# Second feed-forward product in groups of 512 tokens over both batches, with its activations in four fixed buffers, in a fused attention and MLP kernel

## The chip, the cores and the metric

The kernel runs on one core of one Trainium2 chip. The metric is the device time of one execution in microseconds (us). Before the change three runs took 455.62, 456.00 and 456.24 us, so the median is 456.0 us.

## The reference, cut to what matters

Three blocks follow each other: a decaying linear attention, a token-mixing low-rank product with a ReLU feed-forward (`ch`), and a gated MLP. B=2 batches, S=768 tokens, 512 features, 2048 hidden features.

```python
state = gamma * state + einsum('bhd,bhe->bhde', k[:, :, t], v[:, :, t])
y[:, :, t] = scale * einsum('bhd,bhde->bhe', q[:, :, t], state)
...
xt = x.transpose(0, 2, 1)
h = xt @ U @ V
u = x + h.transpose(0, 2, 1)
ch = np.maximum(u @ w_ch1, 0.0) @ w_ch2
x = u + ch
...
h = np.maximum(x @ w_in, 0.0)
u, v = h[..., :d_ff // 2], h[..., d_ff // 2:]
v_s = einsum('ts,bsd->btd', w_spatial, layernorm(v)) + b_spatial[None, :, None]
out = (u * v_s) @ w_out
```

## The kernel before, in words

Activations lie feature-major: `X[b]` is a tile of 128 partitions by four feature blocks by 768 tokens. T = 384 tokens is half a batch. A product in full precision is made of three matmuls (`triple`): each operand is split into a high and a low part of type fp32r, and high times high, high times low and low times high are added in one PSUM bank. A high part is a cast on ScalarE, a low part a subtraction on VectorE or GpSimd.

**Attention.** It runs per pair of heads, eight pairs (four for each batch). A pair loads `q`, `k` (feature-major, named `h` in the load list) and `v`, and for most pairs also `kk`, the same keys token-major; pairs in `TURNED` instead transpose `k` on TensorE (`scale`, L414) and scale the result on its way out of PSUM (L419). `scores` makes the score banks `sc`, masks them into `pt` on VectorE (L451) or on ScalarE and GpSimd (`VIA`, L448 and L449), and forms the chunk states `ds` and their scan `s` (L461). `mix` makes `x` from `pt`, `v`, `q` and `s`; `turn` transposes `x` (`t`, L502), `down` and `up` are the low-rank product (`g`, `gt`, `hu`).

**Feed-forward.** The 2048 hidden features are taken in eight steps `m` of 256. `ch1(m, b)` computes them for one batch; from m = 1 on as a `quad`, seven products of half-size operands (named 1, 5, 6, 7, 2, 4, 3) in four banks qa, qb, qc and qd. Its results leave PSUM in `store(i, h)`, where i is the half of the 256 features and h the half of the tokens. Three of the four are first added to a helper `y` on VectorE (L756), then get their ReLU in place on ScalarE (L757), are cast to the high part (L758) and subtracted for the low part (L759). The fourth goes from the bank with one ScalarE and one VectorE instruction (L753, L754). Each (m, b, i, h) has its own activation tile `a`, taken from the pool "a" of 36 buffers. `ch2(m, b)` then multiplies them with `w2`: for each half h and each of four feature blocks d there are two triples of 384 columns in one bank `acc`, and VectorE adds the bank to `X` (L784).

**The rest.** `gate_u`, `gate_v`, `spatial` and `final` follow with products of 384 and 256 columns.

**What sets the order.** The program first records operations with costs and keys in a `Plan`. `settle` arranges them repeatedly with an event model of the engines, and `give_out` then emits them in the order found. So each engine's program order, also that of SyncE's loads, is fixed in advance by the model's costs. Where the model sees TensorE idle for over 0.5 us before 60 us, `give_out` emits filler matmuls of 384 bf16 columns (`spend`) ahead of the next one; WARM = 11 of them open the program. `SEQ` is the sequence (0,0), (0,1), (1,0), ... (7,1) of (m, b); `ch2` of one element is keyed across the span of the next.

All matmuls are issued at L348 except the transposes.

Of the kernel before, what the change touches and what calls it, by code (L numbers as in the profile page):

```python
# [43 lines left out]
class Plan:  # L44
# [48 lines left out]
    def arrange(self, sizes):  # L93
# [16 lines left out]
        free["D"] = FIRST  # L110
# [189 lines left out]
def pe(n, passes=1):  # L300
    return passes * (10.8 + 0.4219 * n), False
# [3 lines left out]
POOLS = {"a": 36, "w": 24, "raw": 2, "y": 2, "t": 2, "r": 6, "st": 6, "s": 2, "g": 2, "sm": 2, "ps": 8}  # L305
# [16 lines left out]
SUM0, SUM1 = 80.8, 106.2  # L322
VIA = {0: (2,), 1: (), 2: (), 3: (0, 1, 2, 3), 4: (2, 3), 5: (1, 2, 3), 6: (1, 2), 7: (1, 3)}
# [3 lines left out]
TURNED = (0,)  # L327
SEQ = [(m, b) for m in range(NM) for b in range(B)]

STEP = {n: 6 * pe(n)[0] / 1000 for n in (T, DM // 2)}  # L330
# [5 lines left out]
def tile_kernel(ctx: ExitStack, tc: tile.TileContext, a, out: bass.AP):  # L336
    nc = tc.nc
    const = ctx.enter_context(tc.tile_pool(name="const", bufs=1))
    psm = ctx.enter_context(tc.tile_pool(name="psm", bufs=1))
# [16 lines left out]
    sc_t = const.tile([P, 2 * H + NP * (NCH - 1)], F32, name="scales")  # L356
# [13 lines left out]
    X = [const.tile([P, ND, S], F32, name=f"x{b}") for b in range(B)]  # L370

    def xs(b, d, h):
        return X[b][:, d, h * T:(h + 1) * T]
# [54 lines left out]
    def scores(i):  # L428
        b, p = divmod(i, NP)
        for e in range(2):  # L430
            pt_t[i, e] = Buf("a", [P, NCH, P], F32, f"pt{i}{e}")
        for h in range(2):
# [9 lines left out]
            for e in range(2):  # L442
                m = msc[:, 2 * p + e:2 * p + e + 1]

                def pt(e=e, h=h):
                    return pt_t[i, e].t[:, TC * h:TC * h + TC, :]
                if (2 * h + e) in VIA[i]:
                    op({"A": (582, False)}, lambda E, pt=pt, x=sc[e], m=m: E.activation(pt(), x.t, AF.Copy, scale=m), r=[sc[e], "sc"], w=[(pt_t[i, e], h)])  # L448
                    op({"G": gss(T)}, lambda E, pt=pt: E.tensor_mul(pt(), pt(), tri()), r=[(pt_t[i, e], h), TRI], w=[(pt_t[i, e], h)])  # L449
# [614 lines left out]
```

## Time and profile before

| what | before |
|---|---|
| median of three runs | 456.0 us |
| the profiled execution's own time | 454.77 us |
| span of the profiled execution | 453.1 us |
| TensorE busy | 447.2 us (99%) |
| VectorE busy | 396.3 us (87%) |
| ScalarE busy | 257.0 us (57%) |
| GpSimd busy | 126.7 us (28%) |

The span runs from the first to the last instruction; 1.7 us of the profiled time lie around it. "Busy" counts a matmul from its start to its modelled end, and matmuls overlap, so two busy matmuls may follow each other in less than the sum of their durations; the distance between starts is what tells TensorE's pace. The times in all rows are from the span's start. The granted TensorE clock is reported as 1.00 for the whole span.

### The profile page before, as it was taken

Reading aid. Unit: us, or ns where it says so; the run is one execution under the profiler, and the core shown is the slowest. Engines: PE = TensorE matmul, PEld = TensorE weight load, DVE = VectorE, ACT = ScalarE, POOL = GpSimd, SP = SyncE. Lnnn points to the kernel's source line nnn. Section 1 sums busy time; section 2 is a strip of 40 time slices with the busy share of each in tenths; the row PEclk is TensorE's granted clock in tenths of the full one; section 3 lists DMA queues with packets and bytes.
Section 4 is the critical chain, followed back from the end, with each engine's and each line's share of the span. In section 5 each row is a group of like instructions: output and inputs, shape, how many; then the busy total and the mean of one; then the engine's idle time right before and its main releaser. Section 6 shows DMA issues by size and latency. Waiting matters only on the chain.

```text
span 453.1 us, 8442 instructions
## 1 busy us (share of the span) xinstructions
PE 447.2 (99%) x3235; PEld 434.8 (96%) x3235; DVE 396.3 (87%) x847; ACT 257.0 (57%) x526; POOL 126.7 (28%) x112
## 2 busy tenths in 40 slices
PE   9999999999999999999999999999999999999996
PEld 6888799999999999999999999999999999999996
DVE  2767899999999999989888797899997999999843
ACT  3376775673766675754563554566566778353410
POOL 3076763463834242322131012101410001150000
PEclk9999999999999999999999999999999999999999
DMA  8995412320353341433122012000112022000033
GB/s 299 399 399 192 139 50 93 93 94 10 90 179 95 94 138 50 150 110 107 54 93 81 13 48 87 19 1 1 35 36 72 0 94 93 2 1 1 1 139 139
DMA packets 14151, 42.95 MB, mean 95 GB/s; under 512 B 1696, under 2 KB 2592, under 8 KB 14112
## 3 DMA queue, kind: packets, MB, share of 16 engines
q1 hardware_dynamic: 13968, 42.41, 27.3%
q8 instruction: 25, 0.41, 0.4%
q14 instruction: 14, 0.11, 0.1%
q10 hardware_dynamic: 144, 0.02, 0.0%
HBM read 39.27 MB, written 3.15 MB: 94 GB/s over the span
## 4 chain that ended last, share of the span: by engine, by line
PE 92%; DVE 5%; ACT 1%; POOL 0%; issue 0%; DVEq 0%; ACTq 0%
PE acc L348 29%; PE pz L348 8%; PE x L348 4%; PE c L348 4%; PE sc L348 3%; PE t L502 1%; PE ds L348 1%; DVE s21t L556 1%; DVE f21t L562 1%; PE idle L348 1%; DVE f21b L562 1%; DVE pz L862 1%; DVE x L863 1%; PE q10a L348 1%; PE q50a L348 0%; PE qo11d L348 0%
## 5 line engine op out<-in xcount | busy, mean ns | idle before, releaser
L348 PE MATMUL acc<-a,hw 128*128 128x384 f32 x512 | 130.1, 334 | 0.0
L348 PEld LDWEIGHTS acc<-a,hw 128*128 128x128 f32 x512 | 92.5, 188 | 0.3 <-DVE a L759 0.3
L348 PE MATMUL acc<-a,lw 128*128 128x384 f32 x256 | 85.5, 334 | 0.0
L784 DVE TENSOR_TENSOR x<-acc,x 128x384 f32<-128x384 f32 x128 | 69.3, 550 | 7.5 <-PE acc L348 6.9
L600 POOL TENSOR_TENSOR rw<-rw,tw 128x512 int32<-128x512 int32 x32 | 50.7, 1586 | 82.8 <-DVE rw L598 69.8
L348 PEld LDWEIGHTS acc<-a,lw 128*128 128x128 f32 x256 | 48.1, 188 | 0.0
L757 ACT ACTIVATE y<-y 128x384 f32<-128x384 f32 x42 | 22.0, 523 | 36.9 <-DVE y L756 36.7
L595 ACT ACTIVATE yw<-raww 128x512 f32<-128x512 f32 x32 | 21.6, 676 | 19.7 <-DVE rw L598 15.0
L759 DVE TENSOR_TENSOR a<-y,a 128x384 fp32r<-128x384 f32 x39 | 23.7, 608 | 2.9 <-ACT a L758 2.5
L598 DVE SCALAR_TENSOR_TENSOR rw<-yw,rw 128x512 uint32<-128x512 uint32 x32 | 23.1, 723 | 0.0
L596 ACT ACTIVATE tw<-raww 128x512 int32<-128x512 uint32 x32 | 21.6, 674 | 1.1 <-POOL rw L600 1.0
L600 POOL TENSOR_TENSOR rwo<-rwo,two 128x512 int32<-128x512 int32 x4 | 5.4, 1341 | 60.0 <-DVE rwo L598 60.0
L758 ACT CAST a<-y 128x384 fp32r<-128x384 f32 x42 | 21.5, 513 | 1.0
L449 POOL TENSOR_TENSOR pt<-pt,shared 128x384 f32<-128x384 f32 x14 | 14.2, 1036 | 18.7 <-ACT pt L448 18.6
L348 PE MATMUL pz<-ws,vn 128*128 128x384 f32 x108 | 19.0, 334 | 0.0
L348 PE MATMUL pz<-hws,vn 128*128 128x384 f32 x72 | 18.9, 334 | 0.0
L348 PEld LDWEIGHTS pz<-ws,vn 128*128 128x128 f32 x108 | 18.8, 188 | 0.0
L600 POOL TENSOR_TENSOR rwv<-rwv,twv 128x512 int32<-128x512 int32 x4 | 5.3, 1333 | 30.9 <-DVE rwv L598 12.6
L608 ACT CAST hw<-rw 128x512 fp32r<-128x512 f32 x18 | 11.1, 618 | 4.5 <-POOL rw L600 4.2
L348 PE MATMUL sc<-q,k 64*128 64x128 f32 x192 | 13.4, 281 | 0.0
L597 DVE TENSOR_SCALAR rw<-yw 128x512 uint32<-128x512 uint32 x32 | 13.4, 423 | 0.0
L348 PEld LDWEIGHTS sc<-q,k 64*128 64x128 f32 x192 | 11.7, 187 | 1.6 <-issue 0.7
(1080 smaller groups left out, 1260.6 us busy)
## 6 DMA issues: line engine op xcount, KB each, us to landing
raww<-in_w SPq DMA_DIRECT2D x32, 512.0 KB, 3.6
q<-in_qT SPq DMA_DIRECT2D x8, 384.0 KB, 7.8
k<-in_kT SPq DMA_DIRECT2D x8, 384.0 KB, 7.9
v<-in_v SPq DMA_DIRECT2D x8, 384.0 KB, 7.7
kk<-in_k SPq DMA_DIRECT2D x7, 384.0 KB, 7.8
raws<-in_ws SPq DMA_DIRECT2D x6, 384.0 KB, 3.0
out_y<-out SPq DMA_DIRECT2D x6, 384.0 KB, 2.4
rawwu<-in_wu SPq DMA_DIRECT2D x4, 512.0 KB, 3.5
```

The costliest lines, as they stand in the source:

```text
L348: nc.tensor.matmul(o, l, r, start=start, stop=stop, skip_group_check=True)
L449: op({"G": gss(T)}, lambda E, pt=pt: E.tensor_mul(pt(), pt(), tri()), r=[(pt_t[i, e], h), TRI], w=[(pt_t[i, e], h)])
L595: op({"A": c}, lambda E: E.activation(y.t, words(1).bitcast(F32), AF.Copy, scale=2.0 ** -112), r=whole, w=[y])
L596: op({"A": c}, lambda E: E.activation(t.t, words(0), AF.Copy, scale=2.0 ** -29), r=whole, w=[t])
L597: op({"V": vone(n)}, lambda E: E.tensor_single_scalar(r.t, y.t.bitcast(U32), 3, ALU.logical_shift_left), r=[y], w=[r])
L598: op({"V": vss(n)}, lambda E: E.scalar_tensor_tensor(r.t, y.t.bitcast(U32), 0x80000000, r.t, ALU.bitwise_and, ALU.bitwise_or), r=[y, r], w ...
L600: op({"G": gss(n)}, lambda E: E.tensor_tensor(o().bitcast(I32), r.t.bitcast(I32), t.t, ALU.add), r=[r, t], w=[tok])
L608: op({"A": acp(DM)}, lambda E: E.copy(h.t, f(r.t)), r=[r], w=[h])
L757: op({"A": (525, False)}, lambda E: E.activation(y[0](), y[0](), AF.Relu), r=[y[1]], w=[y[1]])
L758: op({"A": acp(T)}, lambda E: E.copy(t.t[:, 0, :], y[0]()), r=[y[1]], w=[(t, 0)])
L759: op({"V": vss(T), "G": gss(T)}, lambda E: E.tensor_sub(t.t[:, 1, :], y[0](), f(t.t[:, 0, :])), r=[y[1], (t, 0)], w=[(t, 1)])
L784: op({"V": vps(T)}, lambda E, o=o, v=xs(b, d, h): E.tensor_add(v, o.t, v), r=[o, ("X", b, d, h)], w=[("X", b, d, h)])
```

## The change

- `ch2` works on groups. For m = 0 to 6 there are three groups of 512 tokens: group 0 is the first 512 tokens of batch 0, group 1 the first 512 of batch 1, group 2 the last 256 of both. Each group and feature block has two triples of 512 columns and one VectorE addition of 512 columns. For m = 7 the four halves of 384 tokens stay.
- The activations of a step lie in four fixed buffers, `a0h`, `a0l`, `a1h` and `a1l`, which hold both batches and are reused by every m. They come from a new pool "b" of 4, shared with the attention's `pt`, which becomes one tile per pair.
- ReLU goes straight from `y` to the high part on ScalarE. The cast is gone; the low part is max(y, 0) minus high, in one VectorE instruction (no longer GpSimd).
- Group 0 of m is keyed into the span of `ch1(m, 1)`, groups 2 and 1 into that of `ch1(m + 1, 0)`, each `LAGS` = 3.9 after the span's begin.
- Pair 1 joins `TURNED`: its `kk` is no longer loaded, and TensorE transposes its `k`. Load order and load keys change, and the pools too (a 29, b 4, w 21, raw 3).
- The planner multiplies the costs of VectorE, ScalarE and GpSimd by `PAD` = 1.02, lets TensorE begin at 0.78, and emits fewer fillers per hole.
- The last stored half tile is added in two pieces of 192 columns, whose stores go out on the ScalarE and the SyncE queue.

```diff
-POOLS = {"a": 36, "w": 24, "raw": 2, ...}
+POOLS = {"a": 29, "b": 4, "w": 21, "raw": 3, ...}
...
-LOADS = 'q0 h0 v0 k1 gs h1 v1 q1 q2 h2 k2 v2 q3 h3 k3 v3 U V0 V1 w10 w11 q4 ...'.split()
+LOADS = "q0 h0 v0 gs h1 v1 q1 q2 h2 k2 v2 q3 h3 k3 v3 U V0 V1 w10 w11 q4 ...".split()
...
+LAGS = 3.9
+PAD = 1.02
+HEAD, LATER = 16, 9.3
-TURNED = (0,)
+TURNED = (0, 1)
...
-                    idle(int((o.start - free - 200.0) / 320.0) + 1, target[-1])
+                    idle(int((o.start - free - 100.0) / 320.0), target[-1])
...
-    A = {}
+    A = [[Buf("b", [P, B, S], F32R, f"a{i}{x}") for x in "hl"] for i in range(2)]
...
             op({"V": vps(T)}, lambda E: E.tensor_add(y[0](), src.t, add[0]()), r=[src, add[1]], w=[y[1]])
-            op({"A": (525, False)}, lambda E: E.activation(y[0](), y[0](), AF.Relu), r=[y[1]], w=[y[1]])
-            op({"A": acp(T)}, lambda E: E.copy(t.t[:, 0, :], y[0]()), r=[y[1]], w=[(t, 0)])
-            op({"V": vss(T), "G": gss(T)}, lambda E: E.tensor_sub(t.t[:, 1, :], y[0](), f(t.t[:, 0, :])), r=[y[1], (t, 0)], w=[(t, 1)])
+            op({"A": (525, False)}, lambda E: E.activation(hi(), y[0](), AF.Relu), r=[y[1]], w=[th])
+            op({"V": vss(T)}, lambda E: E.scalar_tensor_tensor(lo(), y[0](), 0.0, f(hi()), ALU.max, ALU.subtract), r=[y[1], th], w=[tl])
...
-    def ch2(m, b):
-        for h in range(2):
+    def ch2(m, parts):
+        for part in parts:
+            n = T if isinstance(part, tuple) else DM
+            at = {0: (0, slice(0, n)), 1: (1, slice(0, n)), 2: (slice(0, B), slice(n, S))}[part] if n == DM else ...
             for d in range(ND):
-                o = bank([P, T], f"acc{m}{b}{h}{d}")
+                o = bank([P, n], f"acc{m}{d}{part}"...)
                 for i in range(2):
-                    x = A[m, b, i, h]
+                    xh, xl = A[i]
                     triple(o, i == 0, i == 1, n, ...)
-                op({"V": vps(T)}, lambda E, o=o, v=xs(b, d, h): E.tensor_add(v, o.t, v), ...)
+                op({"V": vps(n)}, add, r=[o] + toks, w=toks)
...
-        prev = None
-        for cur in SEQ + [None]:
-            if cur:
-                ch1(*cur)
-            if prev:
-                ch2(*prev)
-            prev = cur
+        for m, b in SEQ:
+            groups = ([(0, 0), (0, 1)] if m == NM - 1 else [0]) if b else [2, 1]
+            if (m, b) != (0, 0):
+                plan.key = ch[m, b] + LAGS
+                ch2(m if b else m - 1, groups)
+            ch1(m, b)
+        ch2(NM - 1, [(1, 0), (1, 1)])
```

**How the order moves, first place: TensorE in the attention of the first two pairs.** Before, behind the first `x` bank of pair 0 (`pt` tiles 187 and 191 belong to pair 0, `kk_126` to pair 1):

```order
L348 LDWEIGHTS const-bfloat16-1.0
L348 MATMUL x_226<-const-bfloat16-1.0 128x384
L348 LDWEIGHTS const-bfloat16-1.0
L348 MATMUL x_226<-const-bfloat16-1.0 128x384
L348 MATMUL x_226<-pt_187,v_122 64x128
...
L348 MATMUL ds_241<-v_135,kk_126 64x64 x10
```

At the same place in the change (`pt_182` is pair 0, `k_126` and `kk_228` pair 1):

```order
L350 MATMUL x_202<-pt_182,v_120 64x128 x6
L417 MATMUL k_216<-shared,k_126 128x128 x3
L417 MATMUL k_222<-shared,k_126 128x128 x3
L350 MATMUL x_231<-pt_182,v_120 64x128 x6
L350 MATMUL ds_244<-v_130,kk_228 64x64 x10
```

Six transposes of pair 1's keys stand where two fillers stood. Of fillers there are 21 before (11 opening ones, 5 ahead of the first transposes, 2 here, 2 among pair 1's scores, 1 ahead of `hu`) and 15 in the change (11, 2, and 2 ahead of `hu`).

**Second place: TensorE from the end of `ch1(5, 1)` to the first reader of its activations.** `q51d` is the bank of product 3, the quad's last, whose `store(0, 1)` writes half h = 1 of batch 1. Before, `acc_3165` reads half h = 0 (`a_3113`, `a_3154`); the first reader of half 1 comes 46 rows later, after three more banks and three products of `ch1(6, 0)`:

```order
L348 MATMUL q51d<-f01b_1051,hsbw_2412 128x384 x2
L348 MATMUL q51d<-f01b_1051,lsbw_2437 128x384
L348 MATMUL acc_3165<-a_3113,hw_2498 128x384 x2
L348 MATMUL acc_3165<-a_3113,lw_2530 128x384
L348 MATMUL acc_3165<-a_3154,hw_2626 128x384 x2
L348 MATMUL acc_3165<-a_3154,lw_2645 128x384
L348 MATMUL q60a<-f00b_689,hw16a 128x384 x2
```

In the change `acc_2847` still reads group 0, and `acc_2893`, the first bank of group 2, reads what `q51d` has just given:

```order
L350 MATMUL q51d<-f01b_1068,hsbw_2333 128x384 x2
L350 MATMUL q51d<-f01b_1068,lsbw_2437 128x384
L350 MATMUL acc_2847<-a1h,hw_2447 128x512
L350 MATMUL acc_2847<-a1l,hw_2447 128x512
L350 MATMUL acc_2847<-a1h,lw_2489 128x512
...
L350 MATMUL q60d<-f00t_919,lsaw_2598 128x384
L350 MATMUL acc_2893<-a0h,hw_2433 128x512
L350 MATMUL acc_2893<-a0l,hw_2433 128x512
```

Twelve matmuls of 384 columns (`q60a` and `q60d`) and three of 512 stand between the two.

**Third place: VectorE behind the same `q51d`, in the change.** `y_2753` is the quad's helper, `a0l` the low part that `acc_2893` reads:

```order
L759 TENSOR_TENSOR y_2753<-q51d,y_2753 128x384
L796 TENSOR_TENSOR x<-acc_2847,x 128x512
L761 SCALAR_TENSOR_TENSOR a0l<-y_2753,a0h 128x384
L641 TENSOR_TENSOR lsaw_2882<-saw_2647,hsaw_2845 128x512
```

Between the addition that ends the product and the low part stands one addition of 512 columns to `X`. Over the whole program VectorE has 801 rows for 841, ScalarE 487 for 523.

## Rows read from the trace of the kernel before

**Rows 1.** The page, part 1: busy us (share of the span) and instructions.

```profile
PE 447.2 (99%) x3235; PEld 434.8 (96%) x3235; DVE 396.3 (87%) x847; ACT 257.0 (57%) x526; POOL 126.7 (28%) x112
```

**Rows 2.** TensorE's two waits at the end of the attention: us in total, times, longest.

```profile
PE c L348 <- POOL lw L609: 0.6, 1, 0.6
PE hu L348 <- DVE gt L489: 0.5, 1, 0.5
```

**Rows 3.** Timeline of TensorE, 384 columns, then 256: start us, length us, what.

```profile
224.80 0.51 PE L348 MATMUL q51a<-f01b,hw15a 128*128 128x384 f32 x2
...
229.48 0.51 PE L348 MATMUL q51b<-f01t,hsaw 128*128 128x384 f32 x2
351.78 0.28 PE L348 MATMUL qv02c<-hsbwv,f10t 128*128 128x256 f32 x1
...
352.86 0.28 PE L348 MATMUL qv10a<-hwv0a,f11b 128*128 128x256 f32 x1
```

**Rows 4.** The page, part 5: busy us, mean ns of one, idle before.

```profile
L348 PE MATMUL acc<-a,hw 128*128 128x384 f32 x512 | 130.1, 334 | 0.0
...
L784 DVE TENSOR_TENSOR x<-acc,x 128x384 f32<-128x384 f32 x128 | 69.3, 550 | 7.5 <-PE acc L348 6.9
...
L759 DVE TENSOR_TENSOR a<-y,a 128x384 fp32r<-128x384 f32 x39 | 23.7, 608 | 2.9 <-ACT a L758 2.5
L598 DVE SCALAR_TENSOR_TENSOR rw<-yw,rw 128x512 uint32<-128x512 uint32 x32 | 23.1, 723 | 0.0
```

**Rows 5.** Windows: PE, PEld, DVE, ACT, POOL busy (x), clock, DMA share, GB/s.

```profile
40.00:57.00 17.00, 16.41 (x272) 12.97 (x269) 15.35 (x32) 14.04 (x29) 13.63 (x14) 1.00 0.41 126
100.00:130.00 30.00, 30.00 (x175) 30.00 (x174) 29.40 (x60) 17.81 (x35) 16.27 (x14) 1.00 0.25 71
```

**Rows 6.** Timeline of TensorE from the start, and of six later transposes.

```profile
0.84 3.68 PE L348 MATMUL idle<-const-bfloat16-1.0 128*128 128x384 bf16 x11 [0.84 <-PEq L1053]
4.32 1.81 PE L348 MATMUL k<-const-bfloat16-1.0 128*128 128x384 bf16 x5
5.92 1.08 PE L414 MATMUL k<-shared,k 128*128 128x128 f32 x6
6.92 1.61 PE L348 MATMUL sc<-q,k 64*128 64x128 f32 x24
...
11.79 1.61 PE L348 MATMUL sc<-q,k 64*128 64x128 f32 x24
...
41.91 0.87 PE L502 MATMUL t<-shared,x 128*128 128x128 f32 x6
```

**Rows 7.** The chain that ended last, near 19 us: start us, us, what.

```profile
19.02 1.65 PE t L502 x12
```

**Rows 8.** SyncE's loads: issues, and us to landing (of the first k, then of q at 4.10).

```profile
1.24 0.42 SPq L354 DMA_DIRECT2D k<-in_kT  x1
...
DMA to landing us min/median/max: 3.6/3.6/3.6
...
4.10 0.80 SPq L354 DMA_DIRECT2D q<-in_qT  x1
...
DMA to landing us min/median/max: 7.6/7.6/7.6
...
8.08 0.33 SPq L354 DMA_DIRECT2D v<-in_v  x1
...
29.51 0.33 SPq L354 DMA_DIRECT2D kk<-in_k  x1
```

**Rows 9.** Timeline around one activation, VectorE, ScalarE and GpSimd.

```profile
164.25 1.45 POOL L600 TENSOR_TENSOR rw<-rw,tw 128x512 int32<-128x512 int32 x1 [1.85 <-ACT y L489]
164.47 1.79 DVE L609 TENSOR_TENSOR lw<-rw,hw 128x512 fp32r<-128x512 f32 x1
...
170.84 0.54 DVE L756 TENSOR_TENSOR y<-q31d,y 128x384 f32<-128x384 f32 x1
...
171.41 0.53 ACT L757 ACTIVATE y<-y 128x384 f32<-128x384 f32 x1 [0.84 <-DVE y L756]
```

More of the change, by code (lines that the diff above doesn't have):

```diff
@@ L109, in arrange @@
         dma, sent = 0.0, 0
-        free["D"] = FIRST
+        free["D"], free["P"] = FIRST, FIRST
         def add(o):
@@ L368, in ident @@
         return shared.t[:, NP + 1, :]
-    X = [const.tile([P, ND, S], F32, name=f"x{b}") for b in range(B)]
+    X = const.tile([P, B, ND, S], F32, name="x")
     def xs(b, d, h):
-        return X[b][:, d, h * T:(h + 1) * T]
+        return X[:, b, d, h * T:(h + 1) * T]
     q_t, k_t, kk_t, v_t, pt_t, s_t, xtok, g_t = ({} for _ in range(8))
@@ L429, in scores @@
         b, p = divmod(i, NP)
-        for e in range(2):
-            pt_t[i, e] = Buf("a", [P, NCH, P], F32, f"pt{i}{e}")
+        pt_t[i] = Buf("b", [P, 2, NCH, P], F32, f"pt{i}")
         for h in range(2):
@@ L529, in run @@
                         mm(u[z].t, g_t[b].t[rows, :], vst.t[rows, h * T:(h + 1) * T], True, True)
[L530 removed]
+                op({"P": (380, "up")}, run, r=[g_t[b], (vst, h)], w=u)
                 for z in range(2):
@@ L869, in store @@
             t, d, cut = ts[i], 2 * m + i, slice(h * T, (h + 1) * T)
+            if (b, m, i, h) == (B - 1, 1, 0, 1):
+                for z, q in enumerate("ED"):
+                    sl, to = slice(z * T // 2, (z + 1) * T // 2), slice(h * T + z * T // 2, h * T + (z + 1) * T // 2)
+                    op({"V": vps(T // 2)}, lambda E, sl=sl, to=to: E.tensor_add(t.t[:, to], src.t[:, sl], add[0]()[:, sl]), r=[src, add[1]], w=[(t, h, z)])
+                    dma(lambda to=to: out[b, d * P:(d + 1) * P, to], lambda to=to: t.t[:, to], P * T * 2, r=[(t, h, z)], eng=q)
+                return
             if add is None:
@@ L906, in tile_kernel @@
         at = [AT0 + STEP0 * i for i in range(NP)] + [AT1 + STEP1 * i for i in range(NP)]
-        loads = {x: k - 100.0 for k, x in enumerate(LOADS)}
+        loads = {x: k - 100.0 if k < HEAD else LATER + (k - HEAD) * 1.0 for k, x in enumerate(LOADS)}
         for i in range(2 * NP):
@@ L929, in tile_kernel @@
                 up(i // NP)
-        ch, need = {}, {}
+        ch, need, span = {}, {}, {}
         t = CH0
-        for n, (m, b) in enumerate(SEQ):
+        for m, b in SEQ:
             ch[m, b] = t
             need.setdefault(m, t)
-            t += 15 * STEP[T] + (CH1 if n == 0 else 0)
-        gu = t
+            span[m, b] = 7 * STEP[T] + (CH1 if (m, b) == (0, 0) else 0 if (m, b) == (0, 1) else 8 * STEP[T] if m == NM - 1 and b else (8, 4)[b] * STEP[DM])
+            t += span[m, b]
+        gu = t + 8 * STEP[T]
         for m in range(NM):
@@ L943, in tile_kernel @@
             for z in range(2):
-                weight("w2", 2 * m + z, need[m] + (8 + z) * STEP[T] - LEAD, loads.get(f"w2{2 * m + z}"))
+                weight("w2", 2 * m + z, ch[m, 1] + z * STEP[T] - LEAD, loads.get(f"w2{2 * m + z}"))
         for m in range(2):
@@ L955, in tile_kernel @@
             operands(0, b, "t1 t2 t3 t4")
-        prev = None
-        for cur in SEQ + [None]:
-            if cur:
-                plan.key, plan.pace = ch[cur], 15 / 7
-                ch1(*cur)
-            if prev:
-                plan.key, plan.pace = ch[cur] if cur else gu - 7 * STEP[T], 15 / 8 if cur else 1
-                ch2(*prev)
-                if prev[0] == NM - 1:
-                    operands(1, prev[1], LAST)
-            prev = cur
+        for m, b in SEQ:
+            groups = ([(0, 0), (0, 1)] if m == NM - 1 else [0]) if b else [2, 1]
+            if (m, b) != (0, 0):
+                plan.key = ch[m, b] + LAGS
+                plan.pace = (span[m, b] - LAGS) / (4 * len(groups) * STEP[T if m == NM - 1 and b else DM])
+                ch2(m if b else m - 1, groups)
+            plan.key, plan.pace = ch[m, b], span[m, b] / (7 * STEP[T])
+            ch1(m, b)
+        operands(1, 0, LAST)
+        plan.key, plan.pace = gu - 8 * STEP[T], 1
+        ch2(NM - 1, [(1, 0), (1, 1)])
+        operands(1, 1, LAST)
         plan.key, plan.pace = gu, 1
```

66 lines of the change are left out of this document (37 added, 29 removed).

## The prediction

> **What bounds the kernel now.** I read the busy shares first. TensorE is busy for 99% of the span, VectorE for 87% [rows 1]. A busy matmul may still be a slow one, so the timeline of TensorE came next. In the feed-forward 27 matmuls of 384 columns start within 4.68 us, one per 173.3 ns; in the gate nine matmuls of 256 columns start within 1.08 us, one per 120.0 ns [rows 3]. Both paces are columns divided by 2.4 GHz plus 13.3 ns: no gaps, and a fixed part per matmul. So from the first feed-forward matmul to the last one TensorE's own program is the bound. Time can be won there only by fewer matmuls or less fixed part, and elsewhere in the attention, where TensorE's pace is broken. The waits show two places at its end: `hu` waits 0.5 us for `gt`, and the first feed-forward bank waits 0.6 us for the low part of its weights [rows 2]. VectorE is the near second: 29.40 of 30 us busy in a feed-forward stretch [rows 5]. A reader should take from this that VectorE's work costs nothing today, but has 2% to spare where it is fullest.
>
> All sums are made against the profiled execution, 454.8 us; the median of the runs is 456.0, so 1.2 is added at the end.
>
> **Part 1, groups of 512.** Before, `ch2` issues 768 matmuls of 384 columns (8 steps, 2 batches, 2 halves, 4 blocks, 6 each); the listing shows the 512 of them that use the high weights [rows 4]. In the change seven of the eight steps issue 72 of 512 columns instead of 96 of 384: 504 for 672. The columns are the same, so only fixed parts go: 168 times 13.3 ns is **2.2 us less**, all on the path. No matmul of 512 columns is in the trace. From the rows, 13.3 ns at both widths gives 226.7 ns. If the price grew in proportion to that of 384 columns (231.1 ns), the gain would be nothing; if the fixed part vanished (213.3 ns), it would be 9.0 us. I take the line through the two rows, as it fits both without a remainder.
>
> The Trainium skill, page "TensorE: Matmul & The Clock Gate", section "Back-to-back issue gap", puts the fixed part of a warm matmul at 2.5 ns. By that rule part 1 would give only 168 times 2.5 ns, 0.4 us, and my forecast would be 1.8 us later. The trace disagrees: its 173.3 ns at 384 columns would have to be 162.5.
>
> **Part 2, the start.** Sixteen fillers precede the first transposes; five of them stand directly ahead. They take 320 ns each (11 from 0.84 to 4.32, 5 to 5.92 [rows 6]), which is 384 columns at 1.2 GHz, the lower of the two levels, though the profile lists a granted clock of 1.00 there. The change has 13, so the transposes can start at 0.84 + 13 x 0.32 = 5.00; the keys they need land at 1.24 + 3.6 = 4.84 [rows 8]. That is 0.96 earlier. The six transposes took 1.00 us (5.92 to 6.92), while six later ones take about 0.7 us [rows 6], so the level rose during them. Begun earlier, they would run wholly low, at 1.3 us: 0.3 lost. Net 0.65 less.
>
> **Part 3, one load less, six transposes more.** SyncE's loads follow each other at (29.51 - 8.08)/22 = 0.97 us each [rows 8]; they, not SyncE, are the limit. Pair 1's `q` lands at 4.10 + 7.6 = 11.70, and pair 1's scores start at 11.79 [rows 6]: bound by this load. With one load fewer ahead of it, it lands at 10.7. TensorE gets there 0.65 earlier by part 2, gets six transposes more (0.65) and four fillers of 384 columns less (about 0.7 at the pace of [rows 3]). Parts 2 and 3 together can give at most the 0.97 of the load, and at least nothing, if pair 1's keys, now transposed and then scaled by VectorE and ScalarE, are late for `ds`. I take **0.8 less**, nearer the upper end, since both limits move by about as much.
>
> **Part 4, the rest of the attention.** A stretch of twelve transposes takes 1.65 us [rows 7] against 1.3 at the pace of [rows 6]; it waits for `x` to leave PSUM. There are four such stretches. In the change's order scores stand between the halves of two of them, so two times 0.35 goes: **0.7 less**, bounds nothing and 1.4. The wait for `gt` stays: two fillers stand there now for one.
>
> **Part 5, the first feed-forward weights.** Their loads now stand ahead of the last pair's, and their low parts ahead of `up`'s additions on VectorE. The wait of 0.6 us goes [rows 2]: **0.6 less**, bounds nothing and 0.6. Late next is then the second batch's `f01b` on GpSimd, needed 36 matmuls, 6.2 us, later.
>
> **Part 6, the activations.** The ScalarE cast goes 42 times and VectorE gains three low parts (608 ns each [rows 4], 1.8 us in sum) from GpSimd. VectorE's additions become 84 of 512 columns and 16 of 384 for 128 of 384 at 550 ns. One of 512 lies between 550 and the 723 ns of another 512-column instruction [rows 4]; at 700 the sum falls from 70.4 to 67.6. VectorE gets lighter, which today costs nothing, so I set nothing for it. What the edit adds is a closer deadline. In every second phase `acc` reads the quad's last result after 12 matmuls of 384 and 3 of 512: 2.76 us. The chain is 0.16 (a matmul's 334 ns less its pace), an addition of 0.55, ReLU 0.53 beginning 0.03 after it [rows 9]: high part after 1.27. The low part on VectorE stands behind the addition of the bank `acc_2847`, which is ready at 0.68 + 0.16 = 0.84 and takes 0.70, and needs 0.61: 2.15, wanted at 2.76 + 0.23 = 2.99. Slack **0.8 us**; in the other phases, with 3.8 us, 1.9. Before, the reader came 8.3 us later (48 matmuls of 384). The buffers also have to be free before ReLU writes them, but their readers are the groups earlier in TensorE's order, and ScalarE has time (17.8 of 30 us [rows 5]). Cost: nothing while that slack holds.
>
> **Part 7, the end.** Two additions of 192 columns and two stores on two queues replace one of each. The first piece leaves earlier, the second later but with half the bytes: nothing, bounds 0.2 either way.
>
> Sum: -2.2 - 0.8 - 0.7 - 0.6 = -4.3. The profiled execution would take 450.5, the median **451.7 us**.
>
> **Rivals.** I call "same" what lies within 0.2% (0.9 us) of 456.0, about what a measurement of this kernel can tell from no change.
>
> *The activations come too late (slower).* A VectorE instruction that meets a running GpSimd one is stretched: 1.79 us [rows 9] where its kind takes about 0.7. One such meeting behind the quad's last product costs 1.1 - 0.8 = 0.3 us, two cost 1.3. At all seven close deadlines that is 9 us: 460.7. It turns the sign from 0.75 us per deadline on. For it: VectorE and GpSimd are both busiest in m = 1 to 4. Against: VectorE gets lighter, and the low part no longer goes to GpSimd. 0.07.
>
> *Only part 1 comes.* VectorE is busy 15.35 of the attention's last 17 us, GpSimd 13.63 [rows 5]; if they bound its end, parts 2 to 5 are waited away again: 453.8. 0.2.
>
> *The clock rises later.* At the moment of the rise before, TensorE had been on transposes for half a microsecond; now it would be for 1.4. If the rise waits for the scores, their first 24 take about 1.5 us longer at the lower level: 453.2. 0.08. The Trainium skill, same page, section "Part 4: PE-mode transpose", states that transposes do not count as busy for the clock; by that rule this case holds. The trace has the rise during transposes, but they follow five fillers, so it does not decide.
>
> *512 columns cost in proportion.* Part 1 gives nothing: 453.9. 0.06.
>
> *Given back elsewhere.* The whole order is planned anew, and of the later stages (gate, spatial, last product) the trace says only that they have almost no wait to lose. If they open some 4 us of new waits: 455.8. 0.09.
>
> That the groups are not what the text says is excluded: the order has 504 matmuls of 512 columns.
>
> **Numbers.** The forecast keeps 0.5. Faster is forecast, only part 1, late clock and proportional price: 0.84; same 0.09; slower 0.07. The range reaches down by the upper bounds of parts 3 to 5 and 7 (0.2 + 0.7 + 0.2) and a fixed part that is partly hidden, and up past the three slower kinds of faster to 454.8; what is left out is the last case, the slower one and little more.
>
> **What would show it.** Right: matmuls of 512 columns start every 227 ns; first transposes at 5.0; the first feed-forward matmul 1.5 us earlier than before (parts 2 to 4) and no wait for `lw`; no TensorE wait on `a0l` or `a1l`. Wrong: waits of `acc` for VectorE at the start of phases; 231 ns per matmul; first scores at half pace; a first feed-forward matmul as late as before.

## The result, and the profile after

The changed kernel takes **458.39 us** (median of four runs, 458.32 to 458.68); the kernel before took 455.81 beside it on the same chip (455.17 to 456.24). The ratio is 1.0059, with a 95% interval of 1.0042 to 1.0076: slower, by about 2.6 us, where 4.3 us less had been forecast. The profiled execution took 458.35 us, with a span of 456.2. So about 0.4 us of the loss lies outside the span: 2.1 to 2.2 us lie around it in the change's four runs, 1.7 before. No run shows why.

The page of the changed kernel, parts 1 and 4 (busy us, share of the span, instructions; then the shares of the chain that ended last):

```profile
PE 447.5 (98%) x3067; PEld 413.5 (91%) x3067; DVE 397.8 (87%) x811; ACT 240.4 (53%) x488; POOL 131.2 (29%) x120
...
PE 82%; DVE 13%; issue 2%; POOL 1%; ACT 1%; DVEq 0%; POOLq 0%
```

Against [rows 1] TensorE issues 168 matmuls fewer, as meant, and is not a bit less busy. ScalarE lost 17 us, and nobody was waiting for that. VectorE did not get lighter in all, though its additions of `acc` fell from 70.4 to 66.3 us.

The waits of TensorE in the changed kernel (us in total, times, longest):

```profile
PE qv02a L350 <- ACT yv L491: 0.9, 1, 0.9
PE qo00c L350 <- DVE yo L698: 0.9, 1, 0.9
PE idle L350 <- PEq L1074: 0.8, 1, 0.8
PE t L504 <- DVE x L488: 0.8, 1, 0.8
PE qu10c L350 <- DVE yu L698: 0.6, 1, 0.6
PE hu L350 <- ACT gt L491: 0.6, 1, 0.6
PE sc L350 <- DVE x L488: 0.5, 1, 0.5
```

The wait for `lw` [rows 2] is gone. New are two waits for `x` in the attention and one in `gate_u`; those in `gate_v` and `final` stood at 0.2 us each before:

```profile
PE qo00c L348 <- DVE yo L696: 0.2, 1, 0.2
PE qv02c L348 <- DVE yv L696: 0.2, 1, 0.2
```

Starts in TensorE's timeline cut the span into three stretches. "Waits" are distances between starts that are more than 60 ns over the pace of [rows 3]; "pace" is what the other distances sum to above that pace.

| stretch | before | after | difference | waits, before to after | pace, before to after |
|---|---|---|---|---|---|
| to the first feed-forward matmul (`c`) | 56.81 | 58.30 | +1.49 | | |
| first `c` to first `qu` | 249.11 | 248.21 | -0.90 | 1.44 to 0.11 | 0.16 to 2.83 |
| first `qu` to the last matmul | 143.31 | 145.89 | +2.58 | 0.92 to 3.38 | 0.00 to 0.12 |

The sum is +3.17 us between the two profiled executions. The pace column is where the term of 2.2 us went: 168 fixed parts fewer should give 2.24 less, and the pace gives 2.67 back in the middle stretch, so the groups of 512 **cost** 0.4 there. The gain in that stretch is waits (1.33, of which 0.72 is the distance that holds the one for `lw`).

One group of 512 columns between products of 384, TensorE's timeline of the changed kernel (start, length, what):

```profile
227.08 0.33 PE L350 MATMUL q51b<-f01t,lsaw 128*128 128x384 f32 x1
227.26 0.39 PE L350 MATMUL acc<-a0h,hw 128*128 128x512 f32 x1
227.49 0.40 PE L350 MATMUL acc<-a0l,hw 128*128 128x512 f32 x1
227.72 0.40 PE L350 MATMUL acc<-a0h,lw 128*128 128x512 f32 x1
227.96 0.39 PE L350 MATMUL acc<-a1h,hw 128*128 128x512 f32 x1
228.18 0.39 PE L350 MATMUL acc<-a1l,hw 128*128 128x512 f32 x1
228.41 0.40 PE L350 MATMUL acc<-a1h,lw 128*128 128x512 f32 x1
228.65 0.51 PE L350 MATMUL q51c<-f01t,hsbw 128*128 128x384 f32 x2
```

Six starts take 1.39 us, 231.7 ns each, and the steps are uneven (0.22 to 0.24). Over all 504 the mean is 230.7 ns, not 226.7; the 384s of that stage went from 173.4 to 174.4.

In the attention the changed kernel is ahead at first (the start, then the first later transposes at 17.83 instead of 18.95) and behind at the end. TensorE's timeline of the start (against [rows 6]), and of the two places where it loses:

```profile
0.84 3.68 PE L350 MATMUL idle<-const-bfloat16-1.0 128*128 128x384 bf16 x11 [0.84 <-PEq L1074]
4.32 0.82 PE L350 MATMUL k<-const-bfloat16-1.0 128*128 128x384 bf16 x2
5.01 0.85 PE L417 MATMUL k<-shared,k 128*128 128x128 f32 x6
5.79 1.61 PE L350 MATMUL sc<-q,k 64*128 64x128 f32 x24
...
11.15 0.71 PE L350 MATMUL sc<-q,k 64*128 64x128 f32 x8
...
28.38 0.88 PE L504 MATMUL t<-shared,x 128*128 128x128 f32 x6
30.04 1.07 PE L504 MATMUL t<-shared,x 128*128 128x128 f32 x6 [0.79 <-DVE x L488]
...
44.20 1.16 PE L350 MATMUL sc<-q,k 64*128 64x128 f32 x14
45.85 0.93 PE L350 MATMUL sc<-q,k 64*128 64x128 f32 x10 [0.50 <-DVE x L488]
```

VectorE's timeline ahead of the first of these waits, in the changed kernel, and under it the same for the second:

```profile
26.65 0.25 DVE L599 TENSOR_SCALAR rU<-yU 128x192 uint32<-128x192 uint32 x1
26.81 0.35 DVE L599 TENSOR_SCALAR rV<-yV 128x384 uint32<-128x384 uint32 x1
27.08 1.16 DVE L600 SCALAR_TENSOR_TENSOR rU<-yU,rU 128x192 uint32<-128x192 uint32 x1
28.16 1.35 DVE L600 SCALAR_TENSOR_TENSOR rV<-yV,rV 128x384 uint32<-128x384 uint32 x1
29.44 1.01 DVE L488 TENSOR_TENSOR x<-x,shared 128x384 f32<-128x384 f32 x2
...
41.81 3.52 DVE L564 TENSOR_TENSOR f00b<-x,f00b 128x384 fp32r<-128x384 f32 x4
45.25 1.01 DVE L488 TENSOR_TENSOR x<-x,shared 128x384 f32<-128x384 f32 x2
```

Both times work that TensorE needs later stands ahead of the additions to `x`, and part of it is stretched beside GpSimd's `pt`. The first time `pt` runs from 26.92 to 29.10: the conversion of `rU` takes 1.16 us and took 0.35 in the kernel before. The second time it runs from 41.69 to 43.98: the first two of the four low parts of `f00b` take 1.30 and 1.36 us, the last two 0.55 each. `f00b` belongs to the first feed-forward operands. Of its eight low parts, five went to GpSimd before and three to VectorE at 61 us, after the attention; now it is four and four. VectorE's load between the first later transposes and the first `c`, before and changed (PE, PEld, DVE, ACT, POOL busy):

```profile
18.95:56.81 37.86, 37.27 (x662) 31.02 (x662) 28.00 (x56) 27.94 (x58) 24.79 (x25) 1.00 0.71 258
17.83:58.30 40.47, 38.52 (x666) 31.52 (x662) 35.46 (x65) 29.77 (x62) 23.80 (x23) 1.00 0.69 255
```

VectorE was busy 28.00 us there and is now 35.46: 7.5 us have come to it, 4.9 of them the four low parts of `f00b` and two of `lw`. TensorE loses 2.6 us in the stretch, 1.3 of it in the two waits shown. The rest is in small pieces that I can't tie to a single wait: 0.6 us more ahead of the matmuls of the `x` banks, 0.5 ahead of those of `hu`, 0.2 of which is a second filler.

The three late waits follow one pattern. `qv02a` needs a bank that ScalarE empties (`yv`, L491); ScalarE does casts of `vn` first. For `qu10c` and `qo00c` the engine is VectorE, which makes parts of `f11t` and `qwv`, and of `f21t`, first. ScalarE and TensorE in the changed kernel:

```profile
355.25 0.51 ACT L856 CAST vn<-r 128x384 fp32r<-128x384 f32 x1
...
355.66 0.36 ACT L491 COPY yv<-qv02a 128x256 f32<-128x256 f32 x1
...
356.07 0.39 PE L350 MATMUL qv02a<-hwv0a,f10b 128*128 128x256 f32 x1 [0.89 <-ACT yv L491]
```

### The profile page after: what moved, and what is told of

Its sections match the earlier page's. It is cut to its first block, busy times and chain, and to the rows that moved or that the text cites. A ratio compares the mean times of both kernels' runs of the same rounds, so it can differ in the third digit from the quotient of the medians.

```text
span 456.2 us, 8031 instructions
## 1 busy us (share of the span) xinstructions
PE 447.5 (98%) x3067; PEld 413.5 (91%) x3067; DVE 397.8 (87%) x811; ACT 240.4 (53%) x488; POOL 131.2 (29%) x120
## 4 chain that ended last, share of the span: by engine, by line
PE 82%; DVE 13%; issue 2%; POOL 1%; ACT 1%; DVEq 0%; POOLq 0%
PE acc L350 26%; PE pz L350 7%; PE c L350 4%; PE x L350 3%; PE sc L350 2%; PE t L504 1%; DVE s20t L558 1%; DVE f11b L564 1%; PE ds L350 1%; POOL f10t L564 1%; DVE s11t L558 1%; PE idle L350 1%; DVE pz L875 1%; DVE f00b L564 1%; DVE f20t L564 1%
## 5 line engine op out<-in xcount | busy, mean ns | idle before, releaser
L796 DVE TENSOR_TENSOR x<-acc,x 128x512 f32<-128x512 f32 x84 | 57.2, 685 | 8.9 <-PE acc L350 8.1
L350 PE MATMUL acc<-a0l,hw 128*128 128x512 f32 x84 | 33.2, 396 | 0.0
L350 PE MATMUL acc<-a0h,lw 128*128 128x512 f32 x84 | 33.2, 395 | 0.0
L350 PE MATMUL acc<-a1h,lw 128*128 128x512 f32 x84 | 33.1, 394 | 0.0
L350 PE MATMUL acc<-a1l,hw 128*128 128x512 f32 x84 | 33.0, 393 | 0.0
L350 PE MATMUL acc<-a0h,hw 128*128 128x512 f32 x84 | 32.7, 390 | 0.0
L350 PE MATMUL acc<-a1h,hw 128*128 128x512 f32 x84 | 32.7, 389 | 0.0
L350 PEld LDWEIGHTS acc<-a1h,lw 128*128 128x128 f32 x84 | 15.8, 188 | 3.4
L350 PEld LDWEIGHTS acc<-a1h,hw 128*128 128x128 f32 x84 | 15.8, 188 | 3.1
L350 PEld LDWEIGHTS acc<-a0l,hw 128*128 128x128 f32 x84 | 15.8, 188 | 1.1
```

The source lines that it names most:

```text
L350: nc.tensor.matmul(o, l, r, start=start, stop=stop, skip_group_check=True)
L796: E.tensor_add(v, o.t.rearrange("p (b t) -> p b t", b=B) if part == 2 else o.t, v)
```

## The experiments

### What does a matmul of 512 columns cost?

`m_pace` is a small kernel of six-matmul groups, each stage of one width, then with traffic on the banks and in SBUF:

```diff
+        for n in (256, 384, 448, 496, 512):
+            stage(n, 10, "none")
+        for mode in ("vector", "scalar", "sbuf", "both"):
+            for n in (384, 512):
+                stage(n, 14, mode)
```

> A kernel by itself, no part of the reference: triples of fp32r matmuls of 256, 384, 448, 496 and 512 columns, six per bank over six banks, each behind its own weight load, first with nothing beside them, then 384 and 512 columns with VectorE reading the banks, with ScalarE reading them, with VectorE and ScalarE on SBUF alone, and with all of it. Theory (the price grows with the width beyond the line through 256 and 384): 512 columns start every 230 to 232 ns with nothing beside them, 448 near 202, 496 near 224. Rival (the price is that of the other engines' traffic): 227 ns alone, the line of 13.3 ns plus columns at 2.4 GHz, and 230 or more only beside VectorE or ScalarE; 384 columns then rise above 173 there too.

Measured mean distances of starts: 119.8 ns at 256, 173.5 at 384, 227.0 at 512; with VectorE, ScalarE or SBUF traffic beside it 227.2 to 228.0 and 173.6 to 173.9. Both expectations missed: neither a width of 512 alone nor the traffic makes 231. What was left is the mixture of widths, and `m_mix` tries it:

```diff
+        mix((512,), 16)
+        mix((384, 512), 32)
+        mix((384, 384, 512, 512), 32)
+        mix((384,) * 8 + (512,) * 8, 32)
+        mix((256, 512), 24)
+        mix((256, 384), 24)
+        mix((384, 512), 32, True)
+        mix((512,), 24, True)
```

> A small kernel of its own: no part of the reference is computed. Groups of six matmuls in float32r, as in the feed-forward stage, into six banks: all of 384 columns, all of 512, the two in turn (one group each, two groups each, eight groups each), 256 and 512 in turn, 256 and 384 in turn, and with VectorE reading the banks and GpSimd subtracting beside it 384 and 512 in turn and 512 alone. Theory (the mixture of widths is the cost): 512 alone starts every 227 ns, but in turn with 384 every 230 to 231, the 384s at 174 to 175 instead of 173.4, and eight groups of each in a row read as each width alone. Rival (the stage's other engines or its operands are the cost): 227 and 173.4 in turn too, and 230 or more only in the stages with VectorE and GpSimd beside.

| groups of six, in turn | narrow, ns | wide, ns |
|---|---|---|
| 512 alone | | 227.1 |
| 384, 512 | 174.3 | 231.5 |
| two of 384, two of 512 | 175.3 | 230.1 |
| eight of 384, eight of 512 | 173.9 | 227.5 |
| 256, 512 | 118.7 | 231.4 |
| 256, 384 | 118.3 | 174.1 |
| 384, 512, VectorE and GpSimd beside | 174.0 | 231.5 |
| 512 alone, VectorE and GpSimd beside | | 226.7 |

TensorE's timeline of `m_mix`, 512 alone and then in turn with 384:

```profile
36.21 0.39 PE L78 MATMUL b<-xh,wl 128*128 128x512 f32 x1
...
37.57 0.39 PE L78 MATMUL b<-xh,wl 128*128 128x512 f32 x1
46.06 0.39 PE L78 MATMUL b<-xh,wh 128*128 128x512 f32 x1
...
47.45 0.33 PE L78 MATMUL b<-xh,wh 128*128 128x384 f32 x1
```

From the first row to the second are six starts in 1.36 us; from the third to the fourth six in 1.39, the very 1.39 of the changed kernel. The theory holds: a row of one width keeps the line of [rows 3], and the first matmuls after each change of width are dearer (which ones, the last section shows).

`e_blk30` and `e_blk60` test this in the kernel itself (both without the padding, so to be held against `e_pad` below). They pack the due times of the 512 groups, so that several stand in a row:

```diff
-plan.pace = (span[m, b] - LAGS) / (4 * len(groups) * ...)
+plan.pace = 0.3 * (span[m, b] - LAGS) / (4 * len(groups) * ...)   (e_blk60: 0.6)
```

> The change without padding, with the due times of the 512-column groups packed closer (0.3 of their spacing), so that several stand in a row: in the kernel's order the width then changes 48 times from 60 us on instead of 154. Theory (the mixture of widths costs the pace): TensorE's excess over 2.4 GHz and 13.3 ns a matmul, 3.06 us without this edit, falls to 0.9 to 1.6 us; the time lies 1.5 to 2 us under what the order's waits alone would give, 453.7 to 456.5. Rival (what reads and writes beside it sets the pace of the 512s): the excess stays at 2.8 to 3.1 us.

> The same with 0.6 of the spacing: 76 changes of width instead of 154. Theory: the excess at 1.4 to 2.0 us, between the two others; time 454 to 456.5, with its waits read beside it. Rival: the excess stays at 2.8 to 3.1 us.

| | changes of width | mean of a 512, ns | pace over the line, us | TensorE waits from first `c`, us | time, us (ratio, 95%) |
|---|---|---|---|---|---|
| `e_pad` | 154 | 231.0 | 3.06 | 0.33 | 455.70 (0.9993 to 1.0012) |
| `e_blk60` | 76 | 229.5 | 2.18 | 3.21 | 458.12 (1.0049 to 1.0078) |
| `e_blk30` | 48 | 228.3 | 1.74 | 3.69 | 457.16 (1.0028 to 1.0055) |

The excess falls with the changes of width, so the rival is out, but by less than expected (1.4 to 2.0 and 0.9 to 1.6). The traces show why: the 512s of a longer row pay more for the change ahead of them. In the changed kernel three in a row take 16 ns above the line in sum, six 29, nine or more 41. Up to the first `qu` the 512s' part of the excess falls from 2.17 us in `e_pad` to 1.40 and 0.80 in the two others, that of the 384s stays (0.81, 0.69, 0.85). The expected times (454 to 456.5 and 453.7 to 456.5) missed: these two orders have 3 us more waits than `e_pad`, at the banks and at the operands. Whether the packing makes them or only another order is not shown.

### What are the groups worth with their pace?

`e_half` is the change with every `ch2` group a half of 384 tokens; `e_half0` is the same without the padding.

```diff
-            groups = ([(0, 0), (0, 1)] if m == NM - 1 else [0]) if b else [2, 1]
+            groups = [(0, 0), (0, 1)] if b else [(1, 1), (1, 0)]
...
```

> The change with ch2 in halves of 384 tokens for every step (16 banks of 384 per step for 12 of 512), all else as in the change; its attention is arranged as in the change. Theory (512 columns bring nothing): within 0.6 us of the change, 457.8 to 459.0, the feed-forward stretch from the first matmul of step 1 to the gate as long as in the change within 0.6. Rival (512 columns do save their fixed part, and something else costs the time): 460.0 or more.

> The change with every ch2 group a half of 384 tokens of one batch (672 matmuls of 384 instead of 504 of 512) and with planned durations that are not padded; to be held against the change without padding (455.7 us). Theory (beside 384-column matmuls the 512-column ones take 230.7 ns, so 504 x 230.7 = 116.3 us against 672 x 173.3 = 116.5 us): TensorE's time is within 1 us either way, 455 to 457. Rival (the groups of 512 are worth the 2.2 us of the prediction and the loss is elsewhere): 457.5 to 458.5. If VectorE's 44 more additions (128 x 550 ns = 70.4 us against 84 x 685 ns = 57.5 us) set the end, then over 459, with waits for VectorE from 60 to 300 us.

`e_half` gave 463.55 us (ratio 1.0151 to 1.0190), 5.2 over the change, which is the rival's range. But 2.6 of it are one wait and 1.7 the lower clock behind it (last section), so its time says nothing on the groups. `e_half0` gave 457.81 (1.0012 to 1.0055), 2.1 above `e_pad`. Its pace lies 0.07 us over the line. From first `c` to the last matmul it takes 392.90 us, of which 2.93 are waits; `e_pad` takes 391.05 with 0.33. So without waits the groups of 512 are 0.75 us *slower* on TensorE, and in this pair of orders they have 2.6 us fewer waits. The page, part 1, of `e_half0` and then `e_pad`:

```profile
PE 446.8 (98%) x3235; PEld 434.8 (95%) x3235; DVE 403.6 (89%) x851; ACT 239.2 (53%) x482; POOL 128.5 (28%) x114
PE 446.1 (98%) x3068; PEld 413.4 (91%) x3068; DVE 392.8 (87%) x808; ACT 241.3 (53%) x487; POOL 130.6 (29%) x124
```

What the groups save is VectorE's time; that the fewer waits come of it is not shown by one pair of orders. The theory was right on TensorE's time (within 1 us) and missed the time in all; the rival's 457.5 to 458.5 came in, but not for its reason, as the groups are not worth 2.2 us on TensorE.

### The padding and the tables

```diff
-PAD = 1.02
+PAD = 1.0      (e_pad; 0.99 in e_p099, 1.01 in e_p101, 1.04 in e_pad4)
```

> The change with PAD = 1.0, all else the same, so the planner counts VectorE, ScalarE and GpSimd as before. Theory (the padding is not the cause): within 1 us of the change, 457.4 to 459.4, TensorE's waits in the gate and the last product still 2 us or more in sum. Rival (the padded durations make the planner order worse): 456.5 or less.

`e_pad` gave 455.70 us, level with the kernel before and 2.7 under the change. Its waits:

```profile
PE t L504 <- DVE x L488: 1.9, 2, 1.1
PE idle L350 <- PEq L1074: 0.8, 1, 0.8
PE k L417 <- DMA k<-in_kT: 0.7, 1, 0.7
PE hu L350 <- ACT gt L491: 0.2, 1, 0.2
PE hu L350 <- DVE gt L491: 0.2, 1, 0.2
```

None is left after the attention: the three late waits belong to the order that the padding draws, not to the groups, the buffers or the loads. The theory (457.4 to 459.4) fell, and the rival came in. That looked like a price of padding, so its other values were run, and the same factor was put on the kernel before (`e_b099`, `e_b101`, `e_b102`: only the planned durations of VectorE, ScalarE and GpSimd times 0.99, 1.01, 1.02).

> The change with the factor on planned durations 0.99 instead of 1.02 (1.00 gave 455.7 us, 1.02 gave 458.4). Theory (any such number makes another order, and orders scatter by 1 to 3 us): 455 to 459, with no line through the factors 0.99, 1.00, 1.01, 1.02, 1.04. Rival (longer planned durations are what makes the order worse, step by step): 455.0 to 455.9, not above the run with 1.00.

> The change with the factor 1.01. Theory (scatter): anywhere from 455 to 460, outside 456.4 to 457.8 as likely as in it. Rival (a steady cost of the padding): 456.4 to 457.8, between the runs with 1.00 and 1.02.

> The change with the factor 1.04. Theory (scatter): 455 to 461, not on the line. Rival (a steady cost of the padding, 2.7 us for each 0.02): 460.5 to 461.8, with more TensorE waits for VectorE's work in the gating and last stages than the change's 3.5 us.

> The kernel before, with the planned durations of VectorE, ScalarE and GpSimd multiplied by 1.02 as the change does, and nothing else. Theory (a padded plan orders the work worse, whatever the kernel): 457 to 459, with new TensorE waits in the gating and last stages. Rival (the padding only shifts the changed kernel from one order to another, and a plan's order scatters by 1 to 3 us with any such number): it may come out on either side, 454.5 to 457, with no more waits in the gating and last stages than before (1.2 us from 306 us on).

> The kernel before, with the planned durations of VectorE, ScalarE and GpSimd multiplied by 0.99, and nothing else. Theory (the kernel before stands at a good draw among orders that scatter by some microseconds, the attention stage above all; its first c at 56.8 us is not a property of its edits): first c at 57.5 to 60 us, time 457 to 461. Rival (the change's own edits of the attention stage cost the 1.5 us): first c at 56.3 to 57.3, time 455 to 456.5.

> The kernel before, with those planned durations multiplied by 1.01. Theory (scatter): first c at 58 to 63, time 457 to 462. Rival (the edits of the change): first c at 56.3 to 57.3, time 455 to 456.5.

| kernel | factor | time, us | ratio, 95% | first `c` | waits `c` to `qu` | waits from `qu` |
|---|---|---|---|---|---|---|
| before | none | 455.8 | | 56.81 | 1.44 | 0.92 |
| `e_b099` | 0.99 | 460.61 | 1.0082 to 1.0120 | 62.64 | 2.70 | 0.40 |
| `e_b101` | 1.01 | 462.17 | 1.0121 to 1.0152 | 61.97 | 3.19 | 1.36 |
| `e_b102` | 1.02 | 461.91 | 1.0058 to 1.0151 | 63.62 | 2.10 | 0.70 |
| `e_p099` | 0.99 | 456.78 | 1.0014 to 1.0039 | 58.63 | 1.16 | 0.81 |
| `e_pad` | 1.00 | 455.70 | 0.9993 to 1.0012 | 58.74 | 0.22 | 0.11 |
| `e_p101` | 1.01 | 461.42 | 1.0119 to 1.0149 | 59.89 | 2.49 | 3.37 |
| the change | 1.02 | 458.39 | 1.0042 to 1.0076 | 58.30 | 0.11 | 3.38 |
| `e_pad4` | 1.04 | 457.58 | 1.0033 to 1.0062 | 58.80 | 0.50 | 1.76 |

There is no line through the factors, and no rival that asked for one came in. One per cent on planned durations draws another order, and orders lie up to 5.7 us apart in the change and 6.4 in the kernel before. That is wider than I had expected: the times of `e_p101`, `e_b102` and `e_b101` and the first `c` of `e_b099` lie above the theory's ranges. The kernel before is the best of its own four by 4.8 us, and most of the distance lies ahead of the first `c`, which its three neighbours reach 5 to 7 us later; from there to the last matmul they take 392.8 to 394.7 us for 392.4. In all three the first `c` waits for an addition of `up` on VectorE (3.1, 1.4 and 1.5 us), a wait that the kernel before does not have and that is at most 0.2 us in the orders of the change. In `e_b099` it is the longest; three fillers follow it, then `c` itself at 62.64:

```profile
61.98 1.12 PE L349 MATMUL c<-const-bfloat16-1.0 128*128 128x384 bf16 x3 [3.06 <-DVE x L534]
```

`e_front` and `e_padfront` put the attention tables and loads of before into the change, with and without padding; `e_port12`, without padding, plans 1.2 times as long those VectorE operations of the attention that the planner keeps from running beside GpSimd.

```diff
-AT0, AT1, CH0, CH1 = 1.0, 20.7, 43.4, 22.3    TURNED = (0, 1)    HEAD = 16    LEAD = 11.4
+AT0, AT1, CH0, CH1 = 1.0, 20.7, 43.5, 22.3    TURNED = (0,)      HEAD = 17    LEAD = 11.1   (and STEP0, STEP1, VIA, LOADS)
```

> The change with the attention's tables of the kernel before: pair 1's keys loaded token-major again, the old list of which score banks go over ScalarE and GpSimd, the old start keys; the groups, buffers and padding stay. Theory (1.5 us of the loss come from the attention's new order, VectorE's conversions and low parts ahead of what TensorE waits for): the first feed-forward matmul at 56.5 to 57.5 instead of 58.3, and 456.8 to 457.8 in all. Rival (the attention's tables are not what costs; the padding or the shared pool does): the first feed-forward matmul at 58 or later, 458 or more.

> The change without the padding, and with the attention tables and the loads of before. Theory (the due times of the attention stage, moved for the padded plan, cost the 1.5 to 1.9 us by which the first matmul of the feed-forward stage is late): first c at 56.5 to 57.5 us of the span, time 453.5 to 454.5, under both kernels. Rival (the stage is late because of what stayed of the change there: one pt buffer for two heads and three kinds of pools of other sizes): first c at 58 to 59, time 455 to 456.5.

> The change without the general padding; only the planned durations of those VectorE operations of the attention stage that share their read port with GpSimd are multiplied by 1.2 (in the trace of the changed kernel one such conversion took 1.16 us beside GpSimd and 0.35 before). Theory (the attention stage is late because the plan puts such operations just ahead of the additions that the transposes wait for): the waits of the t transposes for x (1.9 us in the run without padding) fall under 0.5, first c at 56.5 to 57.7, time 453.7 to 454.8. Rival (the lateness is spread over the stage): first c at 58.2 to 59.2 again, time 455.3 to 456.5.

They gave 459.03 (1.0061 to 1.0091), 458.75 (1.0026 to 1.0072) and 457.40 us (1.0028 to 1.0058), with first `c` at 58.74, 60.16 and 59.03. None brings 56.8 back, and the waits for `x` stay at 0.8, 1.8 and 1.5 us. My theory on each of the three fell: neither the tables nor those durations alone make the stage late. Of the rivals that of `e_front` came in (58 or later, 458 or more); those of the two others missed in the time.

Last, the planned price of a matmul, without padding: `e_cost0` plans a 512 at the 231 ns it takes, `e_pe` keeps the planner's old fixed part.

```diff
-return passes * (11.3 + 0.4219 * n), False
+return passes * (0.4513 * n if n == 512 else 11.3 + 0.4219 * n), False    (e_cost0)
+return passes * (10.8 + 0.4219 * n), False    (e_pe)
```

> The change without the padding, and with the planned duration of a 512-column matmul set to the 231 ns that the chip takes in this mixture of widths instead of 227.3. Theory (scatter of orders around the change's own mean): 456 to 460, first c at 58 to 60, the pace of TensorE as in the other runs of the change (2.8 to 3.1 us above its 2.4 GHz share of columns plus 13.3 ns). Rival (the wrong price of the 512s makes the plan drift, 2 us by the end, and so makes the waits in the gating and last stages): 454.5 to 455.7, with at most 0.3 us of waits from the first qu on.

> The change without the padding, and with the planned fixed share of a matmul at 10.8 ns as before instead of 11.3. Theory (scatter): 455.5 to 460, first c at 58 to 60. Rival (the plan's faster pace hurts, as TensorE falls behind the plan sooner): over 457.5, with waits of more than 2 us from the first qu on.

456.41 us (1.0005 to 1.0025) with 0.68 us of waits from `qu` on, and 458.33 (1.0036 to 1.0066) with 1.69. A right price does not remove the waits, so that rival fell, while the theory held; `e_pe` is in the band of the scatter, and its rival (over 457.5, more than 2 us of waits) is half met: inconclusive.

## Why the prediction was wrong

- **Part 1 (2.2 less) failed.** I took the price from rows in which all neighbours had the same width, and the line does hold there: 227.0 ns alone. In the kernel the widths alternate and a 512 takes 230.7, next to the proportional price (231.1) that I had given 0.06. Measured from the first `c` on: -2.24 for the fixed parts, +2.79 for the pace, so +0.55 where -2.2 stood in the sum. The 13.3 ns of the line is what the chip shows at three widths. The 2.5 ns that the Trainium skill gives for an isolated matmul ("TensorE: Matmul & The Clock Gate", "Back-to-back issue gap") was rightly left out of the sum.
- **Parts 2 and 3 (0.8 less) held.** Transposes at 5.01 (forecast 5.00) for 5.92, so 0.91 earlier (the 0.96 counted three whole fillers of 0.32), scores of pair 1 at 11.15 for 11.79: 0.64 less, though their load landed 0.9 earlier (10.75 for 11.67), so here the load is no longer the bound. The six transposes took 0.78 us and not 1.3: in the trace's record of the granted clock the higher level begins at 4.98 us, at the end of the fillers, where it began at 6.43 before, among the transposes. Their starts are 0.11 to 0.14 us apart from the first on, where the first two steps took 0.21 each before. So the 0.3 charged for the clock was not paid, and the rival on the clock fell. The Trainium skill's rule on transposes ("Part 4: PE-mode transpose" of that page) stays untested, as fillers precede them.
- **Part 4 (0.7 less) failed.** The four stretches of twelve transposes took 6.87 us before and 7.87 after. The two that got scores between their halves gained nothing by it (1.65 and 1.49 before, 1.81 and 1.61 after), and the second one, with the wait for `x`, went from 1.87 to 2.67. I counted on the scores and did not ask what VectorE would put ahead of `x`.
- **Part 5 (0.6 less) held** at its place: no wait for `lw`. Its price was missed. The early low parts, of `lw` and of `f00b`, now run on VectorE inside the attention, and one of the two new waits stands behind them.
- **Part 6 (nothing) held.** No TensorE wait on `a0l` or `a1l` in the changed kernel, and a 512-wide addition takes 685 ns (700 taken, from [rows 4]). Other orders do have such a wait in a group of 512: 0.5 us for `a0l` in `e_front`, 0.3 in `e_pe`, 0.4 for `a1l` in `e_port12`. So the slack is as thin as I put it. (The 0.9 us for `a0l` in `e_port12` and `e_padfront` stands at step 7, in the halves of 384.) VectorE as a whole did not get lighter, as I had assumed. Nothing shows that ScalarE's 17 us were worth anything.
- **Part 7 held**: 3.8 us from the start of the last matmul to the end of the span, before and after. The 0.4 us outside the span are not from this edit: `e_cost0` and `e_p099` have it too, and 1.7 us lie around their spans.
- **The rival "given back elsewhere" came in part** (0.09), and came with the proportional price: 2.5 us of new waits opened in the last stages, where it had some 4, and the attention lost 2.6 us, where the rival looked for nothing.

The span was forecast 4.3 us shorter and came out 3.2 longer. Of these 7.5 us, 2.8 are the price of the 512s (part 1); 3.0 are the stretch ahead of the first `c`, forecast 1.5 less (parts 2 to 4) and measured 1.5 more; 2.5 are the late waits, for which the sum had nothing. The waits between the first `c` and the first `qu` gave 0.7 more than part 5 had asked for.

The step that failed as a whole is the sum itself: it treats the new order as the old one plus edits. Four orders of the old kernel and eight full-width orders of the new one (`e_cost0`, `e_pe` and `e_port12` with the five of the table) show that small changes to the plan scatter the time by more than the change was to bring, and that the old kernel's order is the best of its four. Their medians are 461.3 and 457.5 us (457.9 for the new one with `e_front`, `e_padfront`, `e_blk30` and `e_blk60`), so the edits could be worth some 4 us against a plan that was not picked; with so few draws, all near one plan on each side, this is not shown. Which edit shortens the attention against `e_b099` to `e_b102`, and why the orders of the change reach the first `c` at 58.3 to 60.2 us and not at 56.8, stays open. No version beat the kernel before; `e_pad` is level with it.

## What to carry to other kernels

Where a planner orders the work, a changed cost re-draws the whole order: compare several draws of both versions before a difference of one per cent is put down to an edit, and never take one tuned draw for the kernel. A matmul's price read in a row of equal widths does not hold where widths alternate, so keep equal widths together when that opens no wait. A term off the path (ScalarE's 17 us) brought nothing that can be seen, while work moved onto the second-busiest engine is paid where that engine feeds the first.

## What the runs showed of the hardware

- After a change of width the first nine matmuls of 512 columns, or the first six of 384, are off the line. With two groups of each in turn (`m_mix`) the nine take 229, 233, 236, 224, 231, 236, 228, 232 and 231 ns from start to start and the later ones 226.7; the six take 171, 175, 178, 185, 176 and 182, the later ones 173.3. That is 41 and 26 ns in sum, and rows of nine or more 512s in the changed kernel have the same 41. Behind a single group of 512 the 384s pay only 4 ns. VectorE and GpSimd beside them change nothing (231.5 in both rows of the table).
- In `m_pace` 448 columns took 206.6 ns and 496 columns 224.4, where the line of [rows 3] gives 200.0 and 220.0; 256, 384 and 512 lie on it.
- In `e_half` TensorE waited 2.6 us in one piece, and the granted clock was then 0.53 in a stretch of 3 us. `e_b099` shows the same behind its wait of 3.06 us (windows of `e_half`, then one of `e_b099`):

```profile
77.00:80.00 3.00, 0.40 (x2) 0.19 (x1) 3.00 (x4) 2.52 (x6) 2.53 (x2) 1.00 0.00 0
80.00:83.00 3.00, 2.98 (x10) 2.81 (x10) 2.00 (x5) 1.91 (x4) 1.55 (x2) 0.53 0.31 81
84.00:87.00 3.00, 3.00 (x19) 3.00 (x18) 1.38 (x3) 0.00 (x0) 0.00 (x0) 1.00 0.36 146
62.00:65.00 3.00, 3.00 (x10) 2.66 (x10) 3.00 (x7) 3.00 (x7) 2.45 (x3) 0.50 0.27 104
```

The traces' records of the granted clock have the lower level (1.2 GHz) from 80.19 to 83.60 us in `e_half` and from 61.62 to 65.03 in `e_b099`. In `e_half` eleven matmuls of 384 columns take 3.57 us from 80.19 on, where the pace of [rows 3] gives 1.91: 1.7 us lost, on top of the wait. In `e_b099` the first seven of `c` take 2.45 us for 1.21, so 1.2 of the 2.70 us that the table lists as its waits are the clock.
